# One matmul a head of 128 weight columns in place of two of 64, in the keys-times-values and numerator products of a linear-attention kernel

## Chip, cores and metric

One core of a Trainium2 chip runs the whole program in one launch. The metric is the device time of one execution in microseconds (us); lower is better. TensorE is called PE here (its weight loads PEld), VectorE DVE, ScalarE ACT, GpSimd POOL and SyncE SP. PSUM is where matmuls write; SBUF holds everything else.

## The reference

Linear attention with random features, and two dense layers behind it; batch 4, 8 heads, 576 tokens, head width 64, 128 features. All in float32.

```python
def phi(x):
    proj = np.einsum('bhsd,md->bhsm', x, omega)
    sq = np.sum(x * x, axis=-1, keepdims=True) / 2.0
    h = proj - sq
    h = h - np.max(h, axis=-1, keepdims=True)
    return np.exp(h) / np.sqrt(m)
q_p, k_p = (phi(q_s), phi(k_s))
kv = np.einsum('bhsm,bhsd->bhmd', k_p, v)
z = np.sum(k_p, axis=2)
num = np.einsum('bhsm,bhmd->bhsd', q_p, kv)
den = np.einsum('bhsm,bhm->bhs', q_p, z)[..., None] + 1e-06
return (num / den).astype(np.float32)
```

The result, as 2304 tokens of width 512, goes through two layers of inner width 2048: `g = h * cos(h)` with `h = x @ w_in`, then `g @ w_out`; and the same with `h * clip(h + 3, 0, 6) / 6`.

## The kernel before, in words

The 2304 tokens are cut into 18 chunks of 128. A batch has 576 tokens, four and a half chunks, so chunks 4 and 13 straddle the border of two batches; `rows(c)` (L434) gives for a chunk the batches in it with their row ranges: one range of 128 rows, or two of 64.

`chunk(kind, c, ...)` (L447) enters the tasks of one chunk of keys (kind "k") or queries ("q"), all of them twice, for the two sets of four heads (`hf`):

- loads of the chunk transposed and in natural layout, and for keys of the values with a column of ones behind each head (65 columns a head; the ones give z);
- `proj` (L499, matmuls at L503): the product with omega, with 64 rows of weights a head, two heads on the two halves of PE's rows; for the chunks in `SQ_SET` `halves` (matmuls at L512) adds the squared norms in the same shape; else DVE and ACT or POOL make them;
- `tops` (L529), `bias1`, `bias2` and `exps` (ACT, L555): the maximum and the exponential;
- for keys `kv` (L564, matmuls at L570): k_p times [v, 1] of four heads, summed over the chunks of a batch in one PSUM bank; `fin` copies the finished sum to SBUF through the helper `rnd` (its ACT line is L401);
- for queries `trq` (transposes at L600), `qt` (ACT copy of the transposed features), `num` (L608, matmuls at L613): the transposed features times [kv, z] of the batch, which gives numerator and denominator of four heads; then DVE's `eps`, `rec`, `norm` (L634), the transposes of the result at L648 and a copy by ACT into the activations `xx`.

In `kv` and `num` the weights of a matmul are 64 columns: each head has two matmuls, for column halves j = 0 and 64, which write PSUM partitions 0 to 63 and 64 to 127. The streamed operand has 65 columns. An f32 matmul of the source runs as two weight loads and two matmul instructions.

The first layer runs on four of its sixteen inner blocks beside attention, directly: `pair_slot` (L830) with matmuls of 256 columns at L846 (in) and L872 (out). The rest of both layers follows as a stage of sums and differences of blocks (`stage`, L949) with matmuls of 384 columns at L1058 and L1196, from about 240 us to the end; its last matmuls stream 192 columns.

The order of all work is made when the program is built. `Plan.order` (L187) simulates the engines with a cost and a due time for each task (the numbers in `add(...)`, moved by the table `BIAS`), and the instructions are issued in the order of that simulation. For PE it also counts planned idle time and puts in small matmuls on zeros (`filler`, L1267, issued at L1272 and L1281). The costs in `add` for `kv` (0.7) and `num` (0.58) stand outside the changed lines.

Of the kernel before, what the change touches and what calls it, by code (L numbers as in the profile page):

```python
# [15 lines left out]
B, H, S, D, M = 4, 8, 576, 64, 128  # L16
# [160 lines left out]
class Plan:  # L177
# [5 lines left out]
    def add(self, name, key, engs, fn, after=(), alloc=None, use=(), soft=()):  # L183
        assert name not in self.tasks, name
        self.tasks[name] = Task(name, len(self.tasks), key + BIAS.get(kind_of(name), 0.0), engs, fn, list(after), alloc, list(use), list(soft))
# [140 lines left out]
def attention_moe_moe2_kernel(  # L326
# [14 lines left out]
    nc = tc.nc  # L341
# [17 lines left out]
    buf = {}  # L359
# [14 lines left out]
    def tile_of(name, shape, dt=F32):  # L374
        buf[name] = held(plan.slot[name], shape, dt)
        return buf[name]

    def bank(name):
        buf[name] = banks[plan.slot[name][1]]
        return buf[name]  # L380
# [18 lines left out]
    def rnd(e, o, i):  # L399
        if e == "a":  # L400
            nc.scalar.activation(out=o, in_=i, func=ACTF.Copy)  # L401
        elif e == "p":
            nc.gpsimd.tensor_scalar(out=o, in0=i, scalar1=1.0, scalar2=0.0, op0=ALU.mult, op1=ALU.add)
        else:
            nc.vector.tensor_copy(out=o, in_=i)
# [28 lines left out]
    def rows(c):  # L434
        b0 = (c * 128) // S
        b1 = (c * 128 + 127) // S
        if b0 == b1:
            return [(b0, 0, 128)]
        r = b1 * S - c * 128
        return [(b0, 0, r), (b1, r, 128)]  # L440

    last_chunk = {b: ((b + 1) * S - 1) // 128 for b in range(B)}
# [4 lines left out]
    def chunk(kind, c, k, exp_after, lead, pr, prev, on_pe=False):  # L447
        u = (kind, c)
        isk = kind == "k"
        X, V, A, SQ, MX = ("xT",) + u, ("v",) + u, ("nat",) + u, ("sq",) + u, ("mx",) + u  # L450
# [95 lines left out]
        for hf in range(2):  # L546
            E = ("e", kind, c, hf)
# [12 lines left out]
        if isk:  # L560
            for hf in range(2):
                E = ("e", kind, c, hf)
                for b, r0, r1 in rows(c):
                    def kv(e, b=b, r0=r0, r1=r1, hf=hf, E=E, first=not kv_parts[b, hf]):  # L564
                        if first:
                            bank(("kv", b, hf))
                        p = buf["kv", b, hf]
                        for h in range(4):
                            for j in (0, 64):
                                nc.tensor.matmul(  # L570
                                    out=p[j:j + 64, 65 * h:65 * h + 65],
                                    lhsT=buf[E][r0:r1, 128 * h + j:128 * h + j + 64],
                                    rhs=buf[V][r0:r1, 65 * (2 * h + hf):65 * (2 * h + hf) + 65],
                                    start=first and h == 0, stop=c == last_chunk[b] and h == 3, skip_group_check=True,
                                )

                    parts = kv_parts[b, hf]
                    name = ("kv", b, hf) if not parts else ("kv", b, hf, c)
                    prev = [parts[-1]] if parts else []
                    add(name, k + 3, {"t": 0.7}, kv, prev, alloc=None if parts else f"kv{hf}",  # L580
                        use=[E, V] + ([("kv", b, hf)] if parts else []))
                    parts.append(name)
                    if c == last_chunk[b] and b == rows(c)[0][0]:
                        def fin(e, b=b, hf=hf):
                            if hf == 0:
                                tile_of(("kvs", b, 0), [128, 2, 260])
                            rnd(e, buf["kvs", b, 0][:, hf, :], buf["kv", b, hf][:, :260])

                        add(("kvs", b, hf), k + 3, {"a": 0.4}, fin, [parts[-1]] + ([("kvs", b, 0)] if hf else []),
                            alloc=None if hf else "kvs", use=[("kv", b, hf)])  # L590
            return

        for hf in range(2):
            E, TP, QT, NUM, RD = ("e", kind, c, hf), ("tp", c, hf), ("qt", c, hf), ("num", c, hf), ("rd", c, hf)

            def trq(e, E=E, TP=TP):
                p = bank(TP)
                for h in range(4):
                    o = slice(128 * h, 128 * h + 128)
                    nc.tensor.transpose(p[:, o], buf[E][:, o], ident)  # L600

            def qt(e, TP=TP, QT=QT):
                rnd(e, tile_of(QT, [128, 512]), buf[TP])

            add(TP, k + 3 + 0.1 * hf, {"t": 0.58}, trq, ["ident"] + ([("tp", c, 0)] if hf else ([("xt", c - 1)] if c else [])), alloc="pt", use=[E])
            add(QT, k + 3.5 + 0.1 * hf, {"a": 0.62}, qt, alloc="qt", use=[TP])

            def num(e, QT=QT, NUM=NUM, hf=hf):  # L608
                p = bank(NUM)
                for h in range(4):  # L610
                    for j in (0, 64):
                        b = (c * 128 + j) // S
                        nc.tensor.matmul(  # L613
                            out=p[j:j + 64, 65 * h:65 * h + 65], lhsT=buf[QT][:, 128 * h + j:128 * h + j + 64],
                            rhs=buf["kvs", b, 0][:, hf, 65 * h:65 * h + 65], start=True, stop=True, skip_group_check=True,
                        )

            add(NUM, k + 4.5 + 0.1 * hf, {"t": 0.58}, num, [("kvs", b, hf) for b, _, _ in rows(c)] + ([("num", c, 0)] if hf else [("tp", c, 1)]), alloc="pt",
                use=[QT] + [("kvs", b, 0) for b, _, _ in rows(c)])

            def eps(e, NUM=NUM, RD=RD):
                rd = tile_of(RD, [128, 8])
                nc.vector.tensor_scalar(out=rd[:, 0:4], in0=buf[NUM][:, D:260:65], scalar1=EPS, scalar2=TWOPI, op0=ALU.add, op1=ALU.mult)

            def rec(e, RD=RD):
                rd = buf[RD]
                nc.vector.reciprocal(out=rd[:, 4:8], in_=rd[:, 0:4])

            def norm(e, NUM=NUM, RD=RD, hf=hf):
                p = buf[NUM][:, :260].rearrange("p (h d) -> p h d", h=4)  # L630
                rd = buf[RD]
                if hf == 0:
                    tile_of(("xn", c, 0), [128, H, D])
                nc.vector.tensor_tensor(  # L634
                    out=buf["xn", c, 0][:, hf:8:2, :], in0=p[:, :, :D],
                    in1=rd[:, 4:8].unsqueeze(2).to_broadcast([128, 4, D]), op=ALU.mult,
                )

            add(RD, k + 5.3, {"v": 0.16}, eps, alloc="rd", use=[NUM])
            add(("rec", c, hf), k + 5.4, {"v": 0.17}, rec, use=[RD])  # L640
            add(("xn", c, hf), k + 5.5, {"v": 0.42}, norm, [("rec", c, hf)] + ([("xn", c, 0)] if hf else []),
                alloc=None if hf else "xn", use=[NUM, RD])
# [718 lines left out]
```

## Time and profile before

| what | value |
|---|---|
| median of 3 runs | 913.63 us (913.43 to 915.17) |
| profiled execution, its own time | 911.47 us |
| its span, first to last instruction | 909.8 us |
| mean granted PE clock | 1.000 |
| matmul instructions on PE | 6972, as many weight loads |

The profile is of one execution. A group of instructions is told by its line, engine and operation; "128*64" before a matmul's operands means 128 rows and 64 columns of weights, "64*128" 64 rows and 128 columns. A timeline row joins neighbouring instructions of one line: its start and the start of the next row tell how long PE needed for them, better than the length of the row, since the ends of matmuls are modelled and overlap.

### The profile page before, as it was taken

The page shows a single profiled execution, that of the slowest core. Times are in us where ns is not written, and L with a number is a line of the kernel's source. Part 1 is how long each engine was busy: PE and PEld are TensorE (multiplying, and loading weights), DVE is VectorE, ACT ScalarE, POOL GpSimd, SP SyncE. Part 2 cuts the span into 40 slices and gives each one's busy share as a digit, 9 for nine tenths or more (in the row PEclk, how much of TensorE's full clock was granted, in tenths as well). Part 3 has the DMA queues.
Part 4 walks back from the last instruction along what each step waited for, and adds up shares of the span by engine and source line. Part 5 has one row for each costly group of instructions (what it writes and reads, how often), then busy time and mean ns, then how long its engine had stood idle before and what let it go on. Part 6 is the DMA issues. An engine that isn't in the chain of part 4 may idle for free.

```text
span 909.8 us, 17405 instructions
## 1 busy us (share of the span) xinstructions
PE 903.4 (99%) x6972; PEld 883.3 (97%) x6972; DVE 638.4 (70%) x1038; ACT 541.8 (60%) x1083; POOL 230.8 (25%) x175
## 2 busy tenths in 40 slices
PE   9999999999999999999999999999999999999998
PEld 7988999999999999999999999999999999999998
DVE  4786896786778788977568789765676667745442
ACT  6998888985486656656456467654544344434320
POOL 3130313325445433322342433112022002200000
PEclk9999999999999999999999999999999999999999
DMA  8645453423677647741545168423932636153412
GB/s 314 217 154 164 143 193 137 162 71 104 222 309 275 213 145 274 281 150 62 229 137 204 42 260 325 190 93 109 382 135 93 259 133 234 47 203 110 191 54 103
DMA packets 44736, 162.02 MB, mean 178 GB/s; under 512 B 4592, under 2 KB 15984, under 8 KB 40560
## 3 DMA queue, kind: packets, MB, share of 16 engines
q1 hardware_dynamic: 44656, 160.92, 48.8%
q8 instruction: 55, 0.90, 0.4%
q14 instruction: 25, 0.20, 0.1%
HBM read 118.43 MB, written 42.47 MB: 177 GB/s over the span
## 4 chain that ended last, share of the span: by engine, by line
PE 96%; DVE 1%; DMA 1%; ACT 1%; issue 1%; SPq 0%; POOL 0%; DVEq 0%; ACTq 0%
PE b L1196 38%; PE b L1058 33%; PE b L846 6%; PE b L872 5%; PE b L503 4%; PE b L570 2%; PE b L613 2%; PE b L600 2%; PE b L512 1%; PE b L648 1%; DMA F<-kT 1%; PE b L1272 0%; DVE R L408 0%; ACT R L401 0%; DVE F L730 0%
## 5 line engine op out<-in xcount | busy, mean ns | idle before, releaser
L408 POOL TENSOR_TENSOR R<-F,R 128x384 fp32r<-128x384 f32 (+3 forms) x103 | 171.0, 1664 | 282.8 <-ACT R L401 253.2
L401 ACT ACTIVATE R<-F 128x768 fp32r<-128x768 f32 (+3 forms) x242 | 173.8, 737 | 101.6 <-PE b L1196 56.5
L1196 PE MATMUL b<-R,R 128*128 128x384 f32 (+1 forms) x1062 | 201.7, 333 | 0.0
L1196 PEld LDWEIGHTS b<-R,R 128*128 128x128 f32 x1062 | 185.1, 188 | 0.0
L1058 PE MATMUL b<-R,R 128*128 128x384 f32 x966 | 183.7, 334 | 0.0
L1196 PE MATMUL b<-R 128*128 128x384 f32 (+1 forms) x966 | 183.2, 333 | 0.0
L1058 PEld LDWEIGHTS b<-R,R 128*128 128x128 f32 x966 | 168.7, 188 | 0.0
L1196 PEld LDWEIGHTS b<-R 128*128 128x128 f32 x966 | 168.4, 188 | 0.0
L1058 PE MATMUL b<-R 128*128 128x384 f32 x798 | 152.8, 334 | 0.0
L1058 PEld LDWEIGHTS b<-R 128*128 128x128 f32 x798 | 139.4, 188 | 0.0
L1223 DVE SCALAR_TENSOR_TENSOR F<-b,F 128x384 f32<-128x384 f32 (+1 forms) x133 | 73.4, 552 | 87.8 <-PE b L1196 86.9
L408 DVE TENSOR_TENSOR R<-F,R 128x384 fp32r<-128x384 f32 (+3 forms) x147 | 126.2, 880 | 11.2 <-ACT R L401 9.3
L1071 ACT ACTIVATE b<-b 128x384 f32<-128x384 f32 x126 | 59.4, 477 | 78.1 <-PE b L1058 77.6
L555 ACT ACTIVATE F<-b,F 128x128 f32<-128x128 f32 x288 | 80.9, 395 | 12.1 <-DVE F L540 10.7
L938 POOL TENSOR_TENSOR F<-F 128x256 f32<-128x256 f32 x40 | 31.4, 798 | 194.7 <-DVE F L736 186.8
L529 DVE TENSOR_REDUCE F<-b 128x4 f32<-128x512 f32 x72 | 47.9, 685 | 34.7 <-PE b L512 18.5
L401 ACT ACTIVATE F<-b 128x512 f32<-128x512 f32 (+2 forms) x104 | 55.5, 549 | 27.4 <-PE b L1058 16.1
L846 PE MATMUL b<-R 128*128 128x256 f32 x432 | 62.1, 290 | 0.0
L872 PE MATMUL b<-R 128*128 128x256 f32 x432 | 58.5, 286 | 0.2 <-ACT F L888 0.2
L846 PEld LDWEIGHTS b<-R 128*128 128x128 f32 x432 | 54.5, 190 | 1.8
L872 PEld LDWEIGHTS b<-R 128*128 128x128 f32 x432 | 54.1, 191 | 0.8 <-ACT F L888 0.4
L503 PE MATMUL b<-F 64*128 64x128 f32 x576 | 42.7, 285 | 0.7 <-DMA F<-kT 0.7
(71 smaller groups left out, 918.2 us busy)
## 6 DMA issues: line engine op xcount, KB each, us to landing
R<-xd SPq DMA_DIRECT2D x77, 768.0 KB, 6.7
F<-w SPq DMA_DIRECT2D x32, 1024.0 KB, 5.3
xd<-R SPq DMA_DIRECT2D x42, 768.0 KB, 4.2
F<-vn SPq DMA_DIRECT2D x18, 260.0 KB, 4.3
F<-qT SPq DMA_DIRECT2D x18, 256.0 KB, 3.1
yy<-F SPq DMA_DIRECT2D x18, 256.0 KB, 2.4
F<-kT SPq DMA_DIRECT2D x17, 256.0 KB, 4.2
F<-qn SPq DMA_DIRECT2D x15, 256.0 KB, 3.7
```

What stands on the lines that cost most here:

```text
L401: nc.scalar.activation(out=o, in_=i, func=ACTF.Copy)
L408: (nc.gpsimd if e == "p" else nc.vector).tensor_tensor(out=o, in0=a, in1=b, op=ALU.subtract)
L503: nc.tensor.matmul(out=buf["pj", kind, c, o][:, 128 * i:128 * i + 128], lhsT=buf[X][64 * o:64 * o + 64, 128 * i:128 * i + 128], rhs=omd[64 ...
L529: nc.vector.tensor_reduce(out=buf[MX][:, o:o + 4], in_=pj, axis=AX.X, op=ALU.min)
L555: nc.scalar.activation(out=p[:, o], in_=pj[:, o], func=ACTF.Exp, scale=-1.0, bias=mx[:, b:b + 1])
L846: nc.tensor.matmul(out=o, lhsT=w[:, 128 * kc:128 * kc + 128], rhs=v, start=(kc == 0 and j == 0), stop=(kc == KC - 1 and j == 2), skip_grou ...
L872: nc.tensor.matmul(out=y, lhsT=w[:, o], rhs=v, start=(first and fi == 0 and j == 0 and ec % 2 == 0), stop=(last and fi == 1 and j == 2 and ...
L938: (nc.gpsimd if e == "p" else nc.vector).tensor_tensor(out=st[:, o:o + 256], in0=x, in1=y, op=op)
L1058: nc.tensor.matmul(out=o, lhsT=a, rhs=v, start=first and kc == 0 and q == 0, stop=kc == 1 and q == 2, skip_group_check=True)
L1071: nc.scalar.activation(out=buf[to][:, 0:NS], in_=buf[frm][:, 0:NS], func=ACTF.Copy)
L1196: nc.tensor.matmul(out=o, lhsT=a, rhs=v, start=q == 0 and not seeded, stop=q == 6 * SWEEP - 1, skip_group_check=seeded)
L1223: nc.vector.scalar_tensor_tensor(out=o, in0=y, scalar=r, in1=o if s else buf[YP].bitcast(F32), op0=ALU.mult, op1=ALU.add)
```

## The change

In `kv` the loop over the column halves goes: one matmul a head takes all 128 columns of weights and writes all 128 partitions. In `num` the loop over the halves becomes a loop over `rows(c)`: one matmul a head with 128 columns where the chunk lies in one batch; in the straddling chunks 4 and 13, whose halves need the sums of different batches, it is two matmuls of 64 columns as before. The costs given to the planner stay.

```diff
@@ -566,13 +566,11 @@
                             bank(("kv", b, hf))
                         p = buf["kv", b, hf]
                         for h in range(4):
-                            for j in (0, 64):
-                                nc.tensor.matmul(
-                                    out=p[j:j + 64, 65 * h:65 * h + 65],
-                                    lhsT=buf[E][r0:r1, 128 * h + j:128 * h + j + 64],
-                                    rhs=buf[V][r0:r1, 65 * (2 * h + hf):65 * (2 * h + hf) + 65],
-                                    start=first and h == 0, stop=c == last_chunk[b] and h == 3, skip_group_check=True,
-                                )
+                            nc.tensor.matmul(
+                                out=p[:, 65 * h:65 * h + 65], lhsT=buf[E][r0:r1, 128 * h:128 * h + 128],
+                                rhs=buf[V][r0:r1, 65 * (2 * h + hf):65 * (2 * h + hf) + 65],
+                                start=first and h == 0, stop=c == last_chunk[b] and h == 3, skip_group_check=True,
+                            )
 
                     parts = kv_parts[b, hf]
                     name = ("kv", b, hf) if not parts else ("kv", b, hf, c)
@@ -608,10 +606,9 @@
             def num(e, QT=QT, NUM=NUM, hf=hf):
                 p = bank(NUM)
                 for h in range(4):
-                    for j in (0, 64):
-                        b = (c * 128 + j) // S
+                    for b, r0, r1 in rows(c):
                         nc.tensor.matmul(
-                            out=p[j:j + 64, 65 * h:65 * h + 65], lhsT=buf[QT][:, 128 * h + j:128 * h + j + 64],
+                            out=p[r0:r1, 65 * h:65 * h + 65], lhsT=buf[QT][:, 128 * h + r0:128 * h + r1],
                             rhs=buf["kvs", b, 0][:, hf, 65 * h:65 * h + 65], start=True, stop=True, skip_group_check=True,
                         )
```

## Rows read from the trace of the kernel before

**Rows 1.** The page: busy shares, and the chain that ended last by engine.

```profile
PE 903.4 (99%) x6972; PEld 883.3 (97%) x6972; DVE 638.4 (70%) x1038; ACT 541.8 (60%) x1083; POOL 230.8 (25%) x175
...
PE 96%; DVE 1%; DMA 1%; ACT 1%; issue 1%; SPq 0%; POOL 0%; DVEq 0%; ACTq 0%
```

**Rows 2.** Busy time by stretch, each engine's instructions in brackets, PEclk the granted clock.

```profile
core 0: us, PE busy (x) PEld busy (x) DVE busy (x) ACT busy (x) POOL busy (x), PEclk, DMA share, GB/s
10.00:40.00 30.00, 29.01 (x559) 26.21 (x560) 20.88 (x30) 27.95 (x85) 9.08 (x6) 1.00 0.88 308
40.00:90.00 50.00, 49.37 (x860) 43.75 (x858) 38.20 (x84) 45.04 (x142) 11.52 (x9) 1.00 0.48 152
90.00:220.00 130.00, 129.74 (x1439) 119.86 (x1438) 100.16 (x218) 105.08 (x224) 42.93 (x34) 1.00 0.40 136
```

**Rows 3.** Waits of PE: us in total, times, the longest.

```profile
PE b L421 <- DVE F L418: 1.2, 1, 1.2
PE b L648 <- DVE F L634: 0.9, 2, 0.6
PE b L503 <- DMA F<-kT: 0.7, 1, 0.7
PE b L512 <- POOL F L476: 0.3, 1, 0.3
```

**Rows 4.** Groups by line and shape: PE's matmuls of the changed lines.

```profile
L613 PE MATMUL b<-F 128*64 128x65 f32 x576 | 24.6, 227 | 0.0
...
L570 PE MATMUL b<-F 128*64 128x65 f32 x512 | 20.2, 225 | 0.0
...
L570 PE MATMUL b<-F 64*64 64x65 f32 x128 | 5.1, 224 | 0.0
```

**Rows 5.** Timeline of PE near 42 us: start, length, line, operands, count.

```profile
41.97 1.10 PE L570 MATMUL b<-F 128*64 128x65 f32 x32
42.90 0.64 PE L613 MATMUL b<-F 128*64 128x65 f32 x16
```

**Rows 6.** Timeline of PE's weight loads at the end, for matmuls of 192 columns.

```profile
904.48 0.75 PEld L1196 LDWEIGHTS b<-R,R 128*128 128x128 f32 x6
905.15 0.75 PEld L1196 LDWEIGHTS b<-R 128*128 128x128 f32 x6
905.82 0.75 PEld L1196 LDWEIGHTS b<-R,R 128*128 128x128 f32 x6
```

**Rows 7.** Timeline of PE near 9 us: eight full-width f32 matmuls.

```profile
8.90 1.16 PE L1281 MATMUL b<-F 128*128 128x128 f32 x8
9.99 0.33 PE L570 MATMUL b<-F 128*64 128x65 f32 x3
```

**Rows 8.** Single lines: durations of f32 weight loads, min/median/max in ns.

```profile
L570 PEld LDWEIGHTS b<-F x640: 129/138/139, 10.0 to 88.0; 128*64 128x64 f32 x128, 64*64 64x64 f32 x32
...
L1272 PEld LDWEIGHTS b<-F x26: 186/191/192, 38.0 to 84.9; 128*128 128x128 f32 x26
```

**Rows 9.** Timeline of PE from 204 to 220 us.

```profile
204.38 0.98 PE L846 MATMUL b<-R 128*128 128x256 f32 x6
205.29 0.69 PE L613 MATMUL b<-F 128*64 128x65 f32 x16
205.91 0.98 PE L846 MATMUL b<-R 128*128 128x256 f32 x6
...
211.76 0.60 PE L648 MATMUL b<-F 128*128 128x128 f32 x4
212.20 0.60 PE L600 MATMUL b<-F 128*128 128x128 f32 x4
...
216.84 0.69 PE L613 MATMUL b<-F 128*64 128x65 f32 x16
...
219.00 0.88 PE L872 MATMUL b<-R 128*128 128x256 f32 x6
219.72 0.60 PE L648 MATMUL b<-F 128*128 128x128 f32 x4
```

## Prediction

> **What bounds the kernel now.** I read the page's busy shares first, then the chain that ended last, then the stages, then PE's waits, and only then single stretches of PE's timeline. The shares put PE at 99% of the span and the chain puts 96% of it on PE [rows 1]. A share that high can hide stalls, because the ends of matmuls are modelled, so the stages come next [rows 2]: in 10 to 40 us PE is busy 29.01 of 30 us, in 40 to 90 us 49.37 of 50, in 90 to 220 us 129.74 of 130, always at a granted clock of 1.00 (the 2.4 GHz level). ACT is second, 27.95 of 30 us and 45.04 of 50 us. What PE waited for in the whole run comes to 3.1 us [rows 3], 1.2 us of it before any work of the two changed lines. So PE's instruction stream is the clock of this kernel: a microsecond added to it before 220 us moves all that follows by about a microsecond.
>
> The changed lines have 576 matmul instructions (L613) and 512 + 128 (L570) [rows 4]. The source has half as many calls: an f32 matmul becomes two loads and two matmuls. A *group* below is one task of four heads, 16 instructions now: 40 groups at L570 (18 chunks by two halves, and two more for each of the two chunks that straddle a batch border), 36 at L613.
>
> **The change part by part.** *Groups that change.* All 40 groups of L570 go from 16 instructions to 8. Of the 36 groups of L613, the four of the straddling chunks keep their 64 columns and their 16 instructions; 32 go to 8. So 72 groups change, 1152 instructions become 576, and each new one loads 128 columns of weights instead of 64 and streams the same 65 columns.
>
> *Price of the old group.* Where two kv groups and a num group follow each other without a change of array shape, two groups take 42.90 - 41.97 = 0.93 us [rows 5], 0.465 us a group or 0.029 us an instruction; so two narrow ones together cost 0.058 us. The column halves evidently run beside each other. 72 groups: 33.5 us.
>
> *Price of the new instruction.* No row shows f32 weights of 128 columns with 65 streamed columns, so I bound it. From below 0.058 us: the stream is the old one, and this is what it costs if the wide load is no dearer than two narrow ones side by side. From above 0.112 + 0.058 = 0.170 us: load and stream in turn, nothing overlapped. Between them the rows decide for the load. The last matmuls of the kernel stream only 192 columns, half of what the others stream, and yet their loads start every (905.15 - 904.48)/6 = 0.112 us [rows 6]. A block of eight f32 matmuls of full width streaming 128 columns takes 1.09 us with a shape change on both sides [rows 7], against 8 x 0.112 = 0.90 us and 0.19 us for the changes. And the load of one f32 instruction lasts 138 ns at 64 columns and 191 ns at 128 [rows 8], 53 ns more for 64 further columns. I take 0.112 us, the row whose stream is shorter than its load; the neighbours are 0.110 (transposes, 0.44/4) and 0.120 (256 columns, 0.72/6) [rows 9]. 576 x 0.1117 = 64.3 us, and 64.3 - 33.5 = **+30.8 us**.
>
> The rate rests on rows of f32r weights and on f32 rows that stream as many columns as they load. The Trainium skill, "TensorE: Matmul & The Clock Gate", section on the back-to-back issue gap, gives a sustained 81 ns for a load and matmul at 128 columns; by that, an estimate, the work would be 46.7 us and the whole sum only 1.6 us slower, and the 0.112 us of rows 6 and 7 speaks against it here.
>
> *Shape changes.* The array's shape (128 x 64, 64 x 64, 64 x 128, 128 x 128) changes where the narrow groups meet their neighbours, and that costs. From 204.38 to 205.91 us PE does six full-width matmuls and one num group in 1.53 us; the six alone take 219.72 - 219.00 = 0.72 us [rows 9] and the group 0.465, so 0.345 us goes into the change in and the change out, 0.172 us each. In PE's timeline the narrow groups stand in 56 stretches, the first at 9.99 us [rows 7], the last at 216.84 us [rows 9], 112 changes. After the edit, 27 stretches lie between full-width neighbours with nothing narrow left (54 changes gone), 9 between a full-width and a 64-row neighbour (one of two gone, 9), and 2 are lone straddling kv groups that take the 64 x 128 shape of their neighbours (4 gone); the other 18 keep both changes, now between full width and 64 rows, or, for four num groups, as before. 67 changes fewer: 67 x 0.172 = **-11.6 us**.
>
> *Waits.* No semaphore wait is added, the order of tasks is the planner's, whose costs the edit does not touch, and no DMA moves. One wait shrinks: L503 waits 0.7 us for the second kT load [rows 3], right behind the first kv group, which becomes some 0.4 us longer: **-0.4 us**. The waits of L648 for DVE (0.9) and of L512 for POOL (0.3) hang on chains that PE itself starts, so I let them stand. ACT and DVE, which read the results, get them later but at a slower pace, and their work in 10 to 90 us does not grow; the 0.112 us a head is the only thing in their way. Halving the instruction count earns nothing by itself: PE is not seen waiting for its queue.
>
> Sum: 30.8 - 11.6 - 0.4 = +18.8 us, nearly all before 90 us: the 40 kv groups and the eight early num groups gain 0.43 us each and lose few changes, while each of the num groups between full-width matmuls gains 0.43 and gives back 0.345. On the profiled execution (911.47 us, span 909.8) that makes 930.3 us; the median of the three runs is 913.63 us, 2.2 us above that execution, and from it the forecast is **932.4 us**.
>
> **The rivals.** *A, faster: the wide load is hidden.* If 128 f32 columns load in the time of two narrow loads side by side, every group keeps its 0.465 us and only the 11.6 us of shape changes are left: 902.0 us. It decides as soon as an instruction costs less than 33.5 + 11.6 = 45.1 us over 576, that is 0.078 us. For it speaks that most f32 rows stream as many columns as they load, so the bound could be the stream. Against it: rows 6, where the stream is short, and the 53 ns of rows 8. The Trainium skill, "TensorEngine Tiling (Array Packing)", key properties, says that changing the tiling mode drains the engine, which speaks for the change; by that rule, the 0.345 us of rows 9 agrees.
>
> *B, loads overlap in part.* The mean of my bound from below and my price, 0.085 us: 49.0 - 33.5 - 11.6 = +3.9, 917.5 us. Little speaks for it; rows 6 keep their beat of 0.112 us over 18 loads.
>
> *C, load and stream in turn.* 0.170 us: 97.9 - 33.5 - 11.6 = +52.8, 966.4 us. Against it: the 128-column streams of rows 7 keep the 0.112 us, so a load does overlap the stream before it.
>
> *D, the freed changes turn into waits.* Entering a num group without a shape change, PE needs the copy of its transposed weights 0.1 to 0.2 us earlier. ACT makes that copy and is busy 105.08 of 130 us in 90 to 220 us [rows 2]. If the 27 full-width stretches give nothing back, 27 x 0.345 = 9.3 us are lost again: 941.7 us. Against it: PE is shown waiting for ACT only for fractions of a microsecond [rows 3].
>
> *E, the edit changes nothing that is executed*, 913.6 us; the counts of rows 4 would stay.
>
> **How the numbers follow.** Chances: forecast 0.85, A 0.03, B 0.03, C 0.03, D 0.05, E 0.01. Inside the forecast the price of an instruction runs from 0.110 (-1.0 us) to 0.120 (+4.8 us), the listed waits could vanish by another 1.2 us, the runs shown spread by 1.7 us, and a change between f32 and f32r neighbours of one shape, which no clean row shows, may cost up to a few microseconds: 928 to 939. I widen it a little on both sides, downwards towards B and upwards to take in most of D: **925 to 941 us**, which leaves out A, B, C, E and the worst of D. No change means here within 0.2%, 1.8 us, about what three runs of this kernel can tell. Faster is A, 0.03; within 0.2% is E and the edge of B, 0.02; slower the rest, 0.95.
>
> **What the profile after would show.** Right: L570 with 320 matmuls and L613 with 320, 64 of them still 64 columns wide; loads of 128 columns of about 190 ns starting every 0.112 us; the first matmul of the w1 stage after attention (L1058) late by most of 18 us, and nothing more lost behind it; by 90 us a delay of some 17 us. Wrong: starts every 0.06 us inside a group (A), of 0.17 us (C), PE idle before L613 with ACT as the releaser (D), or PE waits of over 4 us in all.

## The result and the profile after

The kernel after takes 927.8 us (median of 4 runs, 927.27 to 928.08), the kernel before beside it 914.4 us (4 runs, 913.43 to 915.65): a ratio of 1.0145 with a 95% interval of 1.0127 to 1.0163, slower by 13.4 us. The profiled execution of after took 927.27 us, its span 925.6 us, the granted PE clock 1.000. Against the span of before that is +15.8 us; the two differences are not the same, and the first experiment shows where that comes from.

PE's matmuls of the two lines in the groups by line and shape of the kernel after (L569 was L570, L610 was L613):

```profile
L569 PE MATMUL b<-F 128*128 128x65 f32 x256 | 33.2, 277 | 0.0
L610 PE MATMUL b<-F 128*128 128x65 f32 x256 | 32.4, 270 | 0.0
L569 PE MATMUL b<-F 64*128 64x65 f32 x64 | 7.7, 270 | 0.0
L610 PE MATMUL b<-F 128*64 128x65 f32 x64 | 2.7, 227 | 0.0
```

320 + 320 instead of 640 + 576 [rows 4], the straddling num groups still 64 columns wide. About half the instructions, yet they are busy longer, 76.0 us instead of 49.9. Busy time by stretch, and the chain that ended last by engine (a line of the page):

```profile
10.00:40.00 30.00, 30.00 (x353) 28.47 (x352) 17.97 (x27) 24.74 (x77) 8.72 (x6) 1.00 0.76 252
40.00:90.00 50.00, 49.79 (x548) 46.21 (x548) 36.25 (x75) 39.85 (x120) 10.74 (x8) 1.00 0.45 142
```

```profile
PE 97%; DVE 2%; ACT 1%; issue 1%; DVEq 0%; ACTq 0%
```

PE has even less idle time than before and ACT more: 24.74 of 30 us against 27.95 [rows 2]. PE's waits, in us in total, times and the longest:

```profile
PE b L421 <- DVE F L418: 1.2, 1, 1.2
PE b L869 <- ACT F L885: 0.2, 1, 0.2
PE b L645 <- DVE F L631: 0.2, 1, 0.2
```

The wait for kT and the one of L512 for POOL are gone. At the transposes (L645, before L648) 0.2 us are left of 0.9 [rows 3]: the waits of before at 46 and 171 us are gone, and one at 72 us has come. No wait on ACT has come at the num groups. One thing in this execution is not the edit's: PE's first block of L503, ahead of any changed line, takes from 4.89 to 6.76 us, in before from 4.90 to 6.13, 0.64 us more; why is not shown.

A kv group between 64-row blocks in the timeline of PE, first in before, then in after, and a num group of after between full-width matmuls:

```profile
16.10 0.69 PE L570 MATMUL b<-F 128*64 128x65 f32 x16
16.71 1.16 PE L512 MATMUL b<-F 64*128 64x128 f32 x16
```

```profile
19.55 1.10 PE L569 MATMUL b<-F 128*128 128x65 f32 x8
20.58 1.16 PE L512 MATMUL b<-F 64*128 64x128 f32 x16
```

```profile
209.08 1.00 PE L610 MATMUL b<-F 128*128 128x65 f32 x8
209.89 0.96 PE L843 MATMUL b<-R 128*128 128x256 f32 x6
```

The kv group takes 1.03 us from its start to the next, 0.42 us more than the 0.61 us of the narrow group. The num group takes 0.81 us against 205.91 - 205.29 = 0.62 us before [rows 9], but enters and leaves without a change of shape: with the six matmuls of L843 behind it, it takes 1.60 us to the next num group at 210.68 us, against 1.53 us before, so that the delay along PE's timeline grows by only some 0.08 us at each of these.

### The profile page after: what moved, and what is told of

It is laid out like the page before. It is cut to its first block, busy times and chain, and to the rows that moved or that the text cites. A ratio compares the mean times of both kernels' runs of the same rounds, so it can differ in the third digit from the quotient of the medians.

```text
span 925.6 us, 16252 instructions
## 1 busy us (share of the span) xinstructions
PE 920.9 (99%) x6396; PEld 908.8 (98%) x6396; DVE 638.7 (69%) x1038; ACT 543.2 (59%) x1083; POOL 230.5 (25%) x175
## 4 chain that ended last, share of the span: by engine, by line
PE 97%; DVE 2%; ACT 1%; issue 1%; DVEq 0%; ACTq 0%
PE b L1193 38%; PE b L1055 32%; PE b L843 6%; PE b L869 5%; PE b L503 4%; PE b L569 4%; PE b L610 3%; PE b L598 2%; PE b L512 2%; PE b L645 1%; DVE R L408 1%; PE b L421 0%; PE b L1269 0%; DVE F L529 0%; ACT R L401 0%
## 5 line engine op out<-in xcount | busy, mean ns | idle before, releaser
L408 DVE TENSOR_TENSOR R<-F,R 128x384 fp32r<-128x384 f32 (+3 forms) x147 | 128.2, 894 | 11.2 <-ACT R L401 9.3
L843 PE MATMUL b<-R 128*128 128x256 f32 x432 | 61.7, 289 | 0.0
L843 PEld LDWEIGHTS b<-R 128*128 128x128 f32 x432 | 54.6, 190 | 0.4
L503 PE MATMUL b<-F 64*128 64x128 f32 x576 | 43.1, 288 | 0.0
```

What stands on the lines that cost most here:

```text
L408: (nc.gpsimd if e == "p" else nc.vector).tensor_tensor(out=o, in0=a, in1=b, op=ALU.subtract)
L503: nc.tensor.matmul(out=buf["pj", kind, c, o][:, 128 * i:128 * i + 128], lhsT=buf[X][64 * o:64 * o + 64, 128 * i:128 * i + 128], rhs=omd[64 ...
L843: nc.tensor.matmul(out=o, lhsT=w[:, 128 * kc:128 * kc + 128], rhs=v, start=(kc == 0 and j == 0), stop=(kc == KC - 1 and j == 2), skip_grou ...
```

## The experiments

The first four ran on one chip beside 16 runs of the kernel before (median 913.73 us), the next four beside 13 runs (914.37 us), the last two beside 21 runs (913.81 us).

**e1: the kernel before, profiled again.** No edit.

> The kernel before, unchanged, profiled once more. The one profiled execution of it took 911.47 us, while its other runs took 913.4 to 915.7; the profiled execution of the kernel after took 927.27 us, inside its other runs (927.3 to 928.1). Theory 1 (PE's stream is the clock, and early waits differ from run to run): this execution shows PE's waits before 50 us larger than the 3.1 us of rows 3, by as much as its time is above 911.5 us, and the same starts inside the groups. Rival (the clock or the DMA differs over the whole run): the extra time is spread over the stage from 262 us on.

It took 913.93 us (median of 10), a ratio of 1.0 (0.9989 to 1.001); its profiled execution has a span of 913.4 us, 3.6 us above the first profile. PE's waits in it:

```profile
PE b L648 <- DVE F L634: 2.4, 3, 1.6
PE b L503 <- DMA F<-kT: 1.2, 1, 1.2
PE b L421 <- DVE F L418: 1.2, 1, 1.2
PE b L846 <- issue: 1.1, 1, 1.1
PE b L512 <- POOL F L476: 0.3, 1, 0.3
PE b L872 <- ACT F L888: 0.2, 1, 0.2
```

They sum to 6.4 us, 3.1 us more than before's first profile with its 0.2 us on L872. The longer and the new waits lie at 12 us (kT), 65 us (L648) and 89 us (L846, with no releaser that the profile shows), so only 0.5 us of the excess lies before 50 us, where I had expected all of it; from 97 us on the two executions run in step, 3.65 us apart to the end. So the execution on which the forecast was worked out waited little; the medians of before lie between it and this one (915.11 us).

**e2: only the kv product wide.** The first hunk of the change alone:

```diff
-                            for j in (0, 64):
-                                nc.tensor.matmul(
-                                    out=p[j:j + 64, 65 * h:65 * h + 65],
+                            nc.tensor.matmul(
+                                out=p[:, 65 * h:65 * h + 65], lhsT=buf[E][r0:r1, 128 * h:128 * h + 128],
```

> Only the kv product takes 128 columns; num stays at two matmuls of 64 columns. Theory 1 (0.43 us more for each of 40 groups, 0.172 us back for each shape change saved): profile against profile +12.7 us, nearly all before 90 us. Rival (the loss comes from the queries' side, whose copies are awaited): under +5 us.

924.81 us, ratio 1.0114 (1.0096 to 1.0131), +11.1 us; the span 923.3 us, +13.5 us against the first profile, 0.8 us more than expected.

**e3: only the num product wide.** The second hunk alone:

```diff
-                    for j in (0, 64):
-                        b = (c * 128 + j) // S
+                    for b, r0, r1 in rows(c):
```

> Only the num product takes 128 columns; kv stays at two matmuls of 64 columns. Theory 1: +0.08 us for each of the 24 late groups and +4.1 us for the eight early ones, which now change shape against the narrow kv groups beside them: +6 us, less up to 0.7 us of a wait of L648 for DVE. The two parts then sum to more than the whole change, since kv and num beside each other save changes only together. Rival (num between full-width matmuls gives nothing back, because PE then waits for ACT's copies): +13 us, with PE waits on ACT of several us.

917.05 us, ratio 1.0033 (1.0021 to 1.0045), +3.3 us; the span 916.0 us, +6.2 us, with 0.2 us of PE waits on ACT. The rival's +13 us and its waits did not come. The two parts were expected to sum to more than the whole, since kv and num groups side by side are rid of their shape changes only together: counted with rows and columns, PE has 11 changes fewer in e2, 44 in e3 and 71 in after, and the 16 that are missing would be 2.8 us at 0.172. The spans add 19.7 us where the whole change adds 15.8, but the low first profile stands in that twice. Spans without PE's waits (906.5 us in before, 920.4 in e2, 912.0 in e3, 924.0 in after) add 19.4 us against 17.5, the medians 14.4 against 13.4: the sign is as expected, the size is not settled.

**e4: twice the streamed columns.** In the kernel after, num:

```diff
+                        n = 130 if h < 3 and r1 - r0 == 128 else 65
                         nc.tensor.matmul(
-                            out=p[r0:r1, 65 * h:65 * h + 65], lhsT=buf[QT][:, 128 * h + r0:128 * h + r1],
-                            rhs=buf["kvs", b, 0][:, hf, 65 * h:65 * h + 65], start=True, stop=True, skip_group_check=True,
+                            out=p[r0:r1, 65 * h:65 * h + n], lhsT=buf[QT][:, 128 * h + r0:128 * h + r1],
+                            rhs=buf["kvs", b, 0][:, hf, 65 * h:65 * h + n], start=True, stop=True, skip_group_check=True,
```

> The kernel after, but in the 32 wide num groups three of four heads stream 130 columns instead of 65 (the upper 65 land where the next head's product overwrites them), 192 instructions in all. Theory 1 (a new instruction is paced by its load of 128 columns, 0.112 us): starts stay 0.112 us apart, at most 0.115, and the time is that of the kernel after, +0 to +0.8 us. Rival (paced by the streamed columns): 192 x 0.054 = +10 us and starts some 0.165 us apart.

927.37 us, ratio 1.0144 (1.0126 to 1.0162). The form in the groups, and a group in PE's timeline:

```profile
L611 PE MATMUL b<-F 128*128 128x130 f32 x192 | 27.0, 277 | 0.0
```

```profile
209.89 1.00 PE L611 MATMUL b<-F 128*128 128x130 f32 x8
210.71 0.96 PE L844 MATMUL b<-R 128*128 128x256 f32 x6
```

0.82 us for the eight, against 0.81 with 65 columns. The span is 926.4 us, 0.8 us above after, of which PE's wait for kT alone, 1.2 us here and absent there, is more than the whole. Doubling the stream costs nothing; inside both groups the trace has single starts 0.112 us apart. That was the disputed price, and it rules out a bound by the stream. What is left is the load of 128 columns, and e5 agrees with it: half the columns, half the time.

**e5: the two column halves in turn.** In the kernel before, in kv and likewise in num:

```diff
-                        for h in range(4):
-                            for j in (0, 64):
+                        for h, j in [(h, j) for j in (0, 64) for h in range(4)]:
```

> The kernel before, but in every kv and num group the four heads' matmuls on column half 0 come first and then the four on half 64; the same 16 instructions. Theory 1 (two narrow matmuls cost 0.058 us together because neighbours on different column halves run beside each other): a group needs about twice as long, starts inside a half are 0.055 to 0.06 us apart instead of pairs, 76 groups x 0.4 = +30 us. Rival (a narrow instruction costs 0.03 us by itself, its load being a quarter of a full one's): no difference.

929.07 us, ratio 1.0153 (1.0136 to 1.0169), +14.7 us; the span 927.7 us, +17.9 us. A kv group (L569 here):

```profile
17.28 0.97 PE L569 MATMUL b<-F 128*64 128x65 f32 x16
18.18 1.16 PE L512 MATMUL b<-F 64*128 64x128 f32 x16
```

0.90 us instead of 0.61 for the same 16 instructions. Side by side is shown: with the halves apart, a narrow kernel loses as much as the wide one. The size was missed, by half: +30 us expected. Inside a half the trace has starts 0.058 us apart, twice the old 0.029, as expected; two halves of eight and the same way out would be 1.08 us. The group takes 0.18 us less, because the second half starts at 17.57 us, before the first has ended at 17.74 (starts of single instructions): it overlaps the first at the turn, which I hadn't thought of.

**e6: narrow matmuls for the straddling kv groups.** In the kernel after:

```diff
+                            for j in (0,) if r1 - r0 == 128 else (0, 64):
+                                w = 128 if r1 - r0 == 128 else 64
...
+                                    out=p[j:j + w, 65 * h:65 * h + 65], lhsT=buf[E][r0:r1, 128 * h + j:128 * h + j + w],
```

> The kernel after, but the eight kv groups of the straddling chunks (64 rows) keep two matmuls of 64 columns. Theory 1 (in the kernel after these eight run partly beside the 64-row matmuls of other lines, so they cost 1.5 us less than 0.43 us each and their shape changes): the time changes by -0.6 us only, and the gain per stretch is at the three chains near 30, 75 and 78 us of before. Rival (they cost what the others do): -1.7 us or more.

925.9 us, ratio 1.0119 (1.0104 to 1.0134) where after has 1.0145; the span 923.9 us, 1.7 us less than after. The expectation of -0.6 us fell, and the number of the rival came, though not for its reason. PE's timeline around the first chain of straddling groups, in the kernels before, after and e6 (L571); a joined row bears the shape of its first instruction, and the rows x64, x28 and x48 hold two groups of full chunks between the straddling ones:

```profile
27.85 1.16 PE L503 MATMUL b<-F 64*128 64x128 f32 x16
...
29.83 2.38 PE L570 MATMUL b<-F 64*64 64x65 f32 x64
32.14 1.16 PE L503 MATMUL b<-F 64*128 64x128 f32 x16
```

```profile
30.37 0.37 PE L503 MATMUL b<-F 64*128 64x128 f32 x1
...
32.37 3.57 PE L569 MATMUL b<-F 64*128 64x65 f32 x28
35.67 0.37 PE L503 MATMUL b<-F 64*128 64x128 f32 x1
35.78 0.27 PE L569 MATMUL b<-F 64*128 64x65 f32 x1
```

```profile
30.39 1.16 PE L503 MATMUL b<-F 64*128 64x128 f32 x16
...
32.37 3.23 PE L571 MATMUL b<-F 64*64 64x65 f32 x48
35.52 1.16 PE L503 MATMUL b<-F 64*128 64x128 f32 x16
```

From the L503 block ahead of the chain to the one behind it: 4.29 us before, 5.30 us after (+1.01), 5.13 us in e6 (+0.84). Four groups change there in after and two in e6. By the forecast's terms after should have lost 4 x 0.427 = 1.71 us. e6's two wide groups cost their 2 x 0.427 = 0.85 us to the hundredth, with the straddling groups as they were. In that chain the shape goes from 64 x 64 to 128 x 64 and back in before, and from 64 x 64 to 128 x 128 and back in e6: two changes in each, which I hadn't counted in before since I had taken all narrow groups for one shape. After has two inside the chain as well, between 64 and 128 rows; there the trace has 0.20 us from start to start instead of 0.112. What after is rid of are the two changes between the chain and the 64-row blocks around it, since with 64 rows and 128 columns the straddling groups share the blocks' 64 x 128 shape. And a single L512 or L503 matmul starts between matmuls of the straddling group: the block's matmuls on the other row half run beside them.

**e7: the num groups joined, with a new order.** The late num groups of a chunk as one task in the kernel before:

```diff
+            elif hf == 0:
+                add(NUM, k + 4.5, {"t": 0.01}, lambda e, NUM=NUM: bank(NUM), [("tp", c, 1), ("qt", c, 1)], alloc="pt", use=[QT])
...
+                add(NUM, k + 4.5, {"t": 1.1}, lambda e, num0=num0, num=num, c=c: (num0(e), bank(("num", c, 1)), num(e)),
```

> The kernel before with both halves of the late num groups (chunks 4 to 17) issued in one stretch; the planner makes its order anew. PE has 126 shape changes instead of 157, and 29 matmuls on zeros instead of 24. Theory 1 (0.172 us a change, 0.22 us a matmul on zeros): -5.3 + 1.1 = -4 us against the kernel before. Rival (what a change gives back turns into waits, since the copies and banks are awaited): 0 or slower.

966.21 us, ratio 1.0558 (1.0536 to 1.0579). The longest of PE's waits in it, at a line of the later stage:

```profile
PE b L1066 <- ACT R L401: 20.4, 1, 20.4
```

Instead of 4 us faster it is 51.8 us slower. The new dependency made the planner lay out all engines anew, and 45.7 us of PE's waits, with a granted clock of 0.977 over the run, bury the four microseconds in question. The run says nothing on the price of a shape change; e9 asks again with the order kept.

**e8: the kernel before without the matmuls on zeros.**

```diff
-                    for _ in range(int((now - idle - (FILL_SKIP if ("kvs", B - 1, 1) in done else FILL_SKIP_K)) / T_FILL + 0.5) if f else 0):
+                    for _ in range(0):
```

> The kernel before without the 20 matmuls on zeros that the planner puts where it expects PE to be idle; the order of the rest stays. Theory 1 (PE's stream is the clock and real waits are few): the 40 instructions at 0.112 us go, 4.5 us, and up to 1.5 us of shape changes; waits take some of it back: -2 to -5 us. Rival (they stand where PE would wait anyway): 0, with PE's waits larger by the same 4 us.

915.1 us, ratio 1.0001 (0.9987 to 1.0015): the rival's 0. PE's wait ahead of the transposes, from the timeline, and the stretch around it by engine, with the granted clock as the third number from the end:

```profile
64.15 0.66 PE L648 MATMUL b<-F 128*128 128x128 f32 x4 [2.42 <-DVE F L634]
```

```profile
60.00:70.00 10.00, 7.58 (x115) 6.53 (x111) 7.92 (x18) 6.02 (x20) 3.50 (x2) 0.83 0.43 137
```

The wait of 2.42 us stands where matmuls on zeros and shorter waits had been, and behind it the granted clock falls: it is 0.50 (the 1.2 GHz level) from 65 to 68 us, a mean of 0.83 over these ten microseconds. From the start of L600 behind the wait to the next L613, PE takes 68.41 - 64.64 = 3.77 us where before takes 65.24 - 63.03 = 2.21, 1.6 us more for the same work. PE's waits sum to 7.8 us, 4.5 more than in before's first profile but 1.4 more than in e1's; so waits and the lower clock together took back what the matmuls on zeros had cost, in shares that single executions don't fix.

**e9 and e10: the same join with the order kept.** In the kernel before the finished order is taken, and the first half's num group is issued right before the second half's, its three DVE tasks right behind; e10 does the like for kv where nothing issued between needs the result or its buffers:

```diff
+        for c in range(N_EARLY, NCH):
+            put_off([x for x in (("num", c, 0), ("rd", c, 0), ("rec", c, 0), ("xn", c, 0))], ("num", c, 1))
```

> The kernel before, with its order kept except that in chunks 4 to 17 the first half's num group (and its three DVE tasks) is issued right before the second half's. 131 shape changes instead of 157, the same instructions, the same matmuls on zeros. Theory 1 (a change costs 0.172 us on PE and PE's stream is the clock): 26 x 0.172 = -4.5 us; if the transposes behind them (L648) wait for DVE's three tasks, at most 0.3 us of it comes back per chunk, so -0.5 to -4.5 us. Rival (what a change gives back turns into waits): 0.

> As the run before, and the first half's kv group of a chunk is issued right before the second half's where nothing issued between needs it: 125 shape changes. Theory 1: 6 x 0.172 = 1.0 us less than the run before. Rival: ACT waits for the buffers of the exponentials that are read later, and the time is above that of the run before.

e9 takes 912.6 us, ratio 0.9986 (0.9975 to 0.9996), 1.2 us below the kernel before and inside the expected range. e10 takes 911.64 us, ratio 0.9979 (0.9968 to 0.9991), 2.2 us below the kernel before; it lies 0.96 us below e9, as expected, but the two intervals overlap, so that this last step is not shown. The same work in before and in e9:

```profile
203.18 0.66 PE L600 MATMUL b<-F 128*128 128x128 f32 x4
...
206.72 5.20 PE L872 MATMUL b<-R 128*128 128x256 f32 x42
```

```profile
203.18 0.66 PE L600 MATMUL b<-F 128*128 128x128 f32 x4
...
204.48 1.15 PE L613 MATMUL b<-F 128*64 128x65 f32 x32
...
206.38 5.20 PE L872 MATMUL b<-R 128*128 128x256 f32 x42
```

3.54 us become 3.20 us: 0.34 us for one change in and one out, the price that the forecast had read as 0.345. Of the 4.5 us for 26 changes the medians show 1.2. The stage in which before's two profiles run in step tells where some of the rest went. From the L503 block at 97.36 us to the first L1058 at 237.40, before takes 140.04 us, e1 too (101.01 to 241.05); e9 (98.25 to 236.70) and e10 (97.68 to 236.13) both take 138.45, 1.6 us less. 24 of the 26 changes lie there, 4.1 us at 0.172. L648 waits for DVE at two places of it in e9:

```profile
171.66 0.66 PE L648 MATMUL b<-F 128*128 128x128 f32 x4 [0.97 <-DVE F L634]
190.07 0.66 PE L648 MATMUL b<-F 128*128 128x128 f32 x4 [0.51 <-DVE F L634]
```

In e10 it waits 0.98 and 0.50 us there, in before and e1 only once, 0.25 us. So 1.2 us of what the changes gave back turned into these waits; the remaining 1.3 us are not located.

## Why the forecast was right, and where its sum was off

The forecast said slower, by 18.8 us on PE's stream, with 932.4 us inside 925 to 941; measured 927.8 us, 13.4 us slower. Sign and mechanism are as forecast, and the size was 5.4 us too high. The place is nearly so: L846's matmuls that start at 92.61 us in before start 14.0 us later in after, where some 17 us by 90 us had been forecast; the 1.8 us from there to the end are as forecast.

**PE's stream is the clock: right.** The delay reaches the end undiminished: it is 15.80 us at the first L1058 and 15.8 us over the span, and PE waits less than before.

**The price of an instruction: right.** 0.112 us, taken from a row of f32r weights: single starts lie 0.112 us apart, and of the 1.60 us for eight of them with six of L843, 0.72 us are the six [rows 9], so 0.88 us or 0.110 us each are theirs. A cost for f32 beside f32r neighbours, which the range had allowed for, is not seen in that. e4 shows that the stream doesn't set the pace. The Trainium skill, "TensorE: Matmul & The Clock Gate", section on the back-to-back issue gap, has 81 ns for a load and matmul at 128 columns; the 112 ns inside a group, with 65 streamed columns here and with 130 in e4, do not agree with it for f32 weights, and the measurement decides. Rivals A, B and C fall with these starts, and the stream, which spoke for A, with e4. (The prediction's sums for the 81 ns and for A, B and C leave out its -0.4 us of waits.)

**The narrow pair at 0.058 us: right,** by e5.

**The shape changes: the price right, their worth short.** 0.172 us is confirmed by e9. But "the narrow groups stand in 56 stretches, 112 changes" took 64 x 64 and 128 x 64 for one shape. Counted with rows and columns, the matmuls of PE change shape 161 times in before and 90 times in after, 71 fewer instead of 67. The four more, 0.7 us, belong to the chains with straddling groups near 30, 75 and 78 us: as e6 shows, before pays for the changes inside a chain; after keeps these and is rid of those against the 64-row blocks. Besides, a 64-row kv group in after is no longer a group by itself, since matmuls of L503 and L512 on the other rows run beside it. The stretch with the second and third chain, in before and in after:

```profile
73.67 1.16 PE L503 MATMUL b<-F 64*128 64x128 f32 x16
...
79.69 1.16 PE L503 MATMUL b<-F 64*128 64x128 f32 x16
```

```profile
84.98 1.16 PE L503 MATMUL b<-F 64*128 64x128 f32 x16
...
92.59 1.16 PE L503 MATMUL b<-F 64*128 64x128 f32 x16
```

6.02 us become 7.61, +1.59, where the forecast's terms make 6 x 0.427 - 0.172 = 2.39. At the first chain it is 1.01 instead of 1.71, and at the two lone straddling groups ahead of it nothing (24.44 to 27.85 us in before, 26.97 to 30.37 in after) instead of 2 x 0.427 - 4 x 0.172 = 0.17. Together 2.60 us instead of 4.27, 1.7 us less. That is the whole difference in PE's work: it grew not by the forecast's 30.8 - 11.6 = 19.2 us but by 15.8 us of span and 1.7 us of waits that went, 17.5 us. (In these 17.5 us the first block's 0.6 us is held too, so that elsewhere about as much must be missing; where is not shown.)

**The execution under the sum, and the waits: the step that failed most.** The sum was built on one execution of before, which waited less than the other profiled one, and then added to a median. That is 2.4 us of the 5.4: 15.8 us of span against 13.4 us of medians. Against e1's profile the span grew by 925.6 - 913.4 = 12.2 us with 6.4 - 1.6 = 4.8 us of waits absorbed, again 17.0 us of work; e1's execution is slower than the median of before and the first one faster, and the medians' 13.4 us lies between 12.2 and 15.8.

Another 1.3 us are the waits of the profile itself. "One wait shrinks ... -0.4 us"; I let the waits of L648 and L512 stand because PE starts their chains. They did not stand: PE's waits fell from 3.3 to 1.6 us, 1.7 us instead of 0.4. Of this the 1.0 us at kT and at L512 is at least in part the chance of one execution, whose first block kept PE 0.6 us longer. In e4, with the same kv code, L512 waits 0.3 us for POOL again, and L503 for kT:

```profile
PE b L503 <- DMA F<-kT: 1.2, 1, 1.2
```

Why the waits of L645 shrank is not shown; it may be that PE's other work between the start and the end of such a chain, some of it in the groups that grow, gives the chain more time. Over the profiles PE waits 1.6 to 3.3 us in after, e2, e4, e5 and e6, whose spans are over 13 us longer, and 3.3 to 6.4 us in before, e1, e9 and e10: so a slower PE does wait less, though single executions scatter. The last 1.7 us of the 5.4 are the shape changes above.

**Rival D,** waits for ACT's copies at the num groups, did not come: 0.08 us a late group, and e3.

## What to carry to other kernels

Halving the number of matmuls is no gain where the load of the weights paces them: here two narrow f32 matmuls on different column halves ran beside each other and took 0.058 us together, one wide one 0.112 us, with 65 streamed columns. So compare start-to-start times of both shapes, not instruction counts. Price a change of array shape by itself, count the shapes exactly (rows and columns), and save changes by putting groups of one shape next to each other. Before carrying a sum from one profiled execution to a median, profile the kernel twice and compare the waits; the waits of the bound engine can absorb part of an added cost, and take up part of a saved one (e9).

## What the runs showed that I had not expected

- A matmul on 64 rows overlaps neighbours from other lines on the other row half when both have the 64 x 128 shape: single L503 matmuls start between those of the straddling kv groups (30.37 and 35.67 us in after). Beside the 64 x 64 groups of before and e6 no such start is seen.
- Two column halves issued in turn still overlap at the turn: 0.90 us for a group, between 0.61 us side by side and 1.08 us one after the other.
- Taking out 4.5 us of matmuls on zeros gained nothing: PE waited 2.42 us at one place, and behind it the granted clock was 0.50 from 65 to 68 us, which cost 1.6 us more.
- Behind 97 us two executions of before, 3.65 us apart, keep that distance within 0.01 us, so that stage shows differences of a tenth of a microsecond that whole runs hide (e9 and e10, 138.45 us each).
